# A kernel ordered by a list scheduler: the engine of each PSUM copy made part of the search over orders, and the search continued

## Chip, cores, metric

One NeuronCore of one Trainium2 chip. The metric is the device time of one execution in microseconds (us). TensorE is called PE below, VectorE DVE, ScalarE ACT and GpSimd POOL, as in the profile.

## The reference, cut to what matters

A gated mix of two attention layers over the same x (2048 tokens, 640 wide, 32 heads of 20):

```python
g = sigmoid((x * gate_w).sum(-1, keepdims=True))
a = A(x)   # linear attention: softmax feature maps of q and k, kv = phi_k^T v, normalised by z
b = B(x)   # 4 segments of 512: causal softmax inside a segment, plus a memory M, z of earlier segments
return g * a + (1 - g) * b
```

The arithmetic does not change here: both kernels have the same 3822 matmuls.

## The kernel before: the parts that the argument touches

The program is a graph of 1415 operations, numbered as they are created. A list scheduler in Python orders them when the kernel is built. Each engine then runs its list in that order (in the profile of before VectorE waits 1.76 us for a DMA while a copy whose matmuls ended at 138.9 us stands behind it until 145.08), and the program carries the dependences by semaphores. NUDGE shifts an operation's priority by its number; a smaller `pr` goes earlier.

```python
# Graph.op
o.engs, o.dur, o.fn, o.pr, o.name, o.dma, o.lat = engs, dur, fn, pr + NUDGE.get(len(self.ops), 0.0), name, dma, lat

# Graph.schedule, for every engine e and ready operation o (cut)
s = est(o, e)                      # earliest start: inputs, free PSUM banks, free buffers
if len(o.engs) > 1:                # an operation that two engines could do
    f = s + o.dur[e] - (self.SLACK if e == "pool" else 0.0)
    if any(max(free[x], s) + o.dur[x] < f - 1e-6 for x in o.engs if x != e):
        continue                   # the other engine would be done sooner
# ... of those that can start within DELTA of the earliest, the lowest (pr, idx) wins
```

The only operations with a choice of engine are copies from PSUM, into which this program's matmuls write (`ps` in the profile), to SBUF, where it keeps their operands. There are 113 of them:

```python
def evac(self, n, o, i, W, pr, name="ev", R=(), mode=1):
    op = self.op(("act", "dve"), {"act": d_act(n), "dve": d_dve(n, mode, True)}, None, R=R, W=W, pr=pr, name=name)
    def fn(e):
        if op.stream == "act":
            return e.activation(o(), i(), ACT.Copy)
        return e.tensor_copy(o(), i())
```

Four kinds of operation matter below: the copy of a value tile vA (operation 1113 is that of the 13th tile), the step `pkt1` that reads a transposed key tile pk as soon as its DMA has landed (operation 733), the reduction and the reciprocal of the 14th key tile (1125 and 1126), and the copies of finished output tiles (`out`, for instance 1376). The hole, below, is the idle time of PE at about 144 us, just before the matmuls that need the banks of the 13th value tile.

The softmax here doesn't subtract the row's maximum and nothing guards it: scores larger than these inputs give would overflow.

Of the kernel before, what the change touches and what calls it, by code (L numbers as in the profile page):

```python
# [10 lines left out]
NUDGE = {6: 1.6, 7: 1.65, 8: -2.2, 9: -0.45, 11: -1.7, 19: -3.95, 22: 3, 24: -1.5, 35: -11.8, 36: -2.7, 37: 5.05, 40: 11.15, 62: 0.7, 64: -1.4, 65:  # L11
         -7.8, 66: 0.95, 67: 6.15, 68: 17.2, 69: 9.2, 70: 3.6, 71: 13.15, 72: 2.65, 75: -8.85, 77: 1.3, 93: 4.7, 94: 16.3, 95: -0.65, 97: -1.6, 99:
         -7.9, 101: -10.25, 103: -15.25, 105: 1.1, 106: 9.7, 107: -3.35, 108: -1.55, 109: -0.15, 111: -1.75, 112: 3.45, 113: 0.05, 119: -5.35, 121:
         2.9, 122: 3.2, 124: -5.55, 125: -0.7, 127: 6.1, 129: 3.1, 131: 5.9, 133: -6.55, 135: 5.9, 143: -3.6, 162: -9.4, 163: -4.5, 164: -3.3, 166:
         -9.2, 170: -3.35, 174: 1.85, 179: -5.05, 180: 6, 181: -6.5, 183: -6.3, 187: -3.45, 188: -4.45, 190: -8.2, 192: -2.65, 193: -6.25, 194: -6.6,
         196: -10.35, 200: -0.65, 202: -10.9, 204: -3.1, 205: -2.9, 206: -7.45, 207: -4.25, 208: -8.5, 209: -3.3, 210: -14.45, 211: -7.8, 213: 4.2,
         217: 0.75, 218: -3.2, 219: -10.25, 221: 2.85, 222: -12.25, 223: 42.5, 224: -9.75, 226: -1.55, 230: 0.7, 231: 3.25, 234: -5.6, 235: -1.3, 236:
         5.7, 237: -6.8, 239: -1.75, 241: 6, 243: -0.95, 247: 2.35, 248: 4.6, 249: -4.9, 250: -13.95, 251: 1.2, 252: -9.8, 253: 3.7, 254: 5.35, 256:
         -5.533, 260: -5.3, 269: 1.071, 270: 0.85, 271: -5.1, 273: -4.75, 277: 3.25, 282: 9.4, 283: 6.85, 284: -9.6, 285: 0.95, 286: -8.15, 287: 2.65,
         288: 11.9, 289: -4.05, 290: -0.15, 291: 6.15, 292: 1.452, 293: -1.4, 294: 7.3, 295: 4.35, 296: -1.7, 297: 8.55, 298: -9, 299: -2.3, 300:  # L20
         -5.05, 301: -2.05, 302: 1.6, 303: 1.5, 304: 1.85, 306: -1.25, 307: -4.35, 309: -3.65, 310: 7.4, 311: 0.25, 313: -0.5, 315: 1.4, 319: -1, 321:
         0.7, 322: 3.45, 323: 1.5, 324: -9.9, 325: 4.027, 328: 0.85, 332: 2.7, 333: 5.65, 335: 0.85, 336: 0.5, 337: -2.8, 338: -0.8, 339: 0.85, 341:
         2.8, 344: -3.85, 345: 6, 348: 3.1, 350: 1.35, 352: -1.1, 358: 4.35, 359: 8.25, 360: 4.05, 363: 2.35, 367: 2.55, 368: 8.3, 369: 0.4, 373: 3.9,
         377: -0.7, 383: -0.75, 384: -0.55, 385: -2.35, 386: -0.4, 387: 2.85, 388: 0.05, 389: 3.95, 390: -14.3, 392: 2.6, 397: -7.05, 400: 1.55, 401:
         6.9, 402: 2.35, 403: -2.85, 404: 3.75, 405: -2.9, 407: -0.25, 411: 2.05, 412: 1.75, 413: 3, 415: -0.8, 416: 2.45, 417: -7, 418: -2.65, 419:
         -3.75, 420: -57.2, 421: 10.8, 422: 1.2, 426: 1.55, 430: 3.4, 434: 1.95, 435: 6, 437: -2.15, 438: -1.75, 439: -10.85, 441: -0.8, 445: -0.95,
         446: -2.6, 449: 0.35, 453: 3.75, 455: 10.95, 456: -1.45, 457: -4.15, 458: 7.35, 466: -13.2, 467: -0.9, 468: -2.9, 469: 0.4, 470: 6.4, 471:
         -1.942, 473: -5.4, 475: -1.75, 479: -0.35, 483: -2.15, 484: 0.45, 485: -12, 486: -19.7, 487: -8.75, 488: -8.05, 490: -3.1, 491: -13.85, 492:
         -10.1, 494: 2.6, 498: 3.258, 509: 4.15, 510: -5.5, 511: 9.8, 512: -3.25, 513: -2.6, 514: 8.8, 515: -2.45, 516: 12, 517: 7.6, 518: 1.2, 519:
         -15.923, 521: 0.6, 522: 1.5, 523: -5.35, 524: -0.4, 525: 5.35, 530: -0.035, 531: 0.15, 532: 2.95, 533: -3.8, 534: 0.25, 535: -6.4, 536: 4.8,  # L30
         537: 3.15, 538: 2.672, 539: 14.3, 540: -2, 541: 0.65, 542: 1.4, 543: 6.7, 544: 0.007, 546: 0.5, 547: -9.45, 548: -1.7, 558: 1.65, 559: 4.45,
         561: 4.15, 563: -4.15, 564: 0.1, 565: -1.95, 567: 1.9, 570: 1.8, 571: 0.2, 573: 3.5, 574: 21.8, 576: 4.25, 577: 2.6, 578: 1.5, 579: -9.5,
         581: 3.15, 582: 3.3, 583: 4.4, 584: 10.8, 586: 13.25, 587: 5.9, 590: 0.65, 591: 2.4, 592: 0.35, 594: 10, 596: -4.15, 597: -0.6, 600: 5.4,
         604: -2.4, 605: -0.75, 608: 25.7, 610: -6.8, 611: -6.05, 612: -10.2, 616: -8.4, 619: 6.3, 620: 6.2, 626: -3.8, 627: 3.05, 630: -28.25, 631:
         -13.3, 634: 3, 635: -8.65, 636: 5.15, 638: 2.55, 639: 0.85, 647: 11.35, 649: 1.85, 653: -2.35, 654: -1.35, 658: 3.6, 659: 3.5, 660: -3.322,
         662: -15.35, 664: -3.3, 668: -1.45, 672: 7.55, 673: 10.05, 678: 4.9, 679: -2.05, 683: -2.2, 687: -2.95, 688: 2.05, 690: 10.05, 693: 4.75,
         694: -2.55, 696: -3.55, 698: -2.6, 702: -2.45, 706: -1.65, 707: -6, 710: -8.75, 712: 14.75, 713: -2.8, 715: 3.15, 717: -3.7, 721: 1.45, 722:
         -5.1, 725: -8.9, 726: 0.25, 727: 6.4, 728: 5.1, 733: 0.35, 734: 2.7, 735: 18.4, 736: 8.7, 737: 6.55, 738: 22.45, 739: 0.8, 740: 11.5, 741:
         8.3, 742: 2.2, 743: 7.75, 744: 7.6, 745: -4.95, 746: 5.7, 747: -3, 748: 2.8, 753: 2.45, 755: -0.35, 757: 7.5, 759: 0.674, 760: -6.65, 761:
         0.3, 763: -0.5, 764: 2.35, 765: 7, 767: 3.5, 768: 5.5, 769: 5.75, 770: 2.8, 771: -1.45, 781: 2.2, 784: 0.45, 787: 16.15, 790: -7.7, 791:  # L40
         -0.85, 794: 1.6, 800: 14.35, 801: 7.1, 802: 4.15, 803: 21, 804: 12.15, 805: 6.2, 806: 2.45, 807: 5.2, 809: 18.6, 810: 4.05, 811: 9.2, 812:
         8.95, 813: 19.25, 814: 4.35, 816: 6.15, 817: 9.1, 819: -1.1, 823: -3.9, 827: -1.3, 828: -1.9, 834: 2.15, 835: -5.85, 838: 2.35, 842: 9.2,
         843: -0.45, 845: 54.95, 849: 0.7, 850: -5.8, 853: -1.4, 857: -6.05, 860: 15.5, 861: 3.05, 862: 2.2, 865: 6.6, 867: 26.85, 868: -6, 869: 3.15,
         872: -12.3, 876: 3.95, 877: 4.1, 881: 10.1, 882: 3.85, 883: -1.35, 885: 6.9, 887: 3.35, 891: -1.95, 895: -3.45, 896: -11.95, 900: 6.05, 902:
         -2.5, 903: 12.15, 904: -5.35, 906: -3.85, 910: -10.45, 911: -2.4, 917: 0.05, 919: 7, 921: -0.85, 925: -12.75, 929: 7.15, 930: 6.35, 936:
         1.45, 938: 1.25, 946: 4.95, 951: -2.5, 952: -9.6, 953: -7.2, 955: 4.85, 959: -3.7, 961: -3.5, 962: -2.4, 963: 2.15, 967: -1.85, 968: 14.1,
         969: 6.35, 970: -4.6, 971: 0.5, 972: -3.95, 973: 0.95, 975: -2.55, 976: 14.9, 977: -5.4, 979: 9.25, 981: 0.1, 982: -4.7, 983: -4.75, 984:
         0.85, 985: -7.75, 988: 4.1, 990: -1.75, 991: 1.45, 992: 0.45, 995: 1.8, 999: 0.65, 1001: 9.85, 1003: -0.65, 1004: 4.7, 1005: 5.1, 1006: -6.1,
         1007: 4.2, 1008: 0.85, 1009: 0.4, 1010: 5.15, 1011: 2.85, 1012: 1.35, 1013: 1, 1014: -1.3, 1015: -1.15, 1016: 7.5, 1018: 10.8, 1019: 12.05,
         1020: -0.4, 1021: -9.8, 1022: -3.95, 1023: 0.8, 1024: 5, 1025: 5.85, 1026: -1.05, 1027: 3.6, 1029: -1.9, 1031: 0.3, 1034: 2.6, 1035: 1.45,  # L50
         1036: -10.55, 1037: 3.55, 1038: 12.15, 1040: -0.65, 1041: 5.25, 1042: -0.5, 1045: 0.9, 1047: -3.8, 1048: 8, 1051: 3, 1052: -4.4, 1053: -5.6,
         1054: -1.9, 1055: 1.8, 1056: -0.4, 1058: -2.9, 1059: 1.115, 1061: -0.15, 1062: 2.05, 1063: -1.7, 1064: -3.5, 1065: 5.3, 1066: -0.9, 1067:
         -7.6, 1068: 4.85, 1069: -2.2, 1070: -0.25, 1072: -6.9, 1073: 1.9, 1075: -2.2, 1076: -0.6, 1077: 0.1, 1078: -3.05, 1079: 3.3, 1080: 2.464,
         1081: 1.75, 1083: -1.1, 1084: 1.9, 1087: -3.75, 1088: -8.6, 1090: 5.25, 1091: 2.85, 1092: 2.25, 1095: 1.95, 1097: -5.7, 1098: 1.95, 1101:
         8.85, 1103: 0.4, 1104: 3.4, 1105: -7.75, 1106: -0.15, 1107: -4.85, 1108: -3.45, 1109: 1.55, 1112: 1.85, 1113: 8, 1114: 2.95, 1115: -0.7,
         1116: 5.8, 1118: -1.35, 1119: -1.1, 1120: 0.75, 1123: 0.9, 1127: 7.2, 1129: 3.95, 1130: 0.65, 1131: 1.3, 1133: -4.3, 1134: 1.5, 1136: -2.35,
         1137: 1.7, 1138: 5.9, 1140: 3.05, 1142: 0.35, 1145: 1, 1146: -1.25, 1147: -7.1, 1148: -5.5, 1151: 8.2, 1152: 17.25, 1153: 0.4, 1154: 1.55,
         1155: 8.55, 1156: -2.5, 1157: -8.7, 1158: -2.8, 1161: -4.65, 1168: -4.15, 1170: -3.35, 1171: 7.5, 1173: -3.45, 1175: -3.7, 1176: -5.15, 1177:
# [110 lines left out]
class Graph:  # L169
# [34 lines left out]
    def schedule(self):  # L204
# [147 lines left out]
        while done < n:  # L352
            best = None
            for e in STREAMS:
# [5 lines left out]
                for o in L:  # L360
# [5 lines left out]
                    if len(o.engs) > 1:  # L366
                        f = s + o.dur[e] - (self.SLACK if e == "pool" else 0.0)
                        if any(max(free[x], s) + o.dur[x] < f - 1e-6 for x in o.engs if x != e):
                            continue
# [12 lines left out]
            s, e, o = best  # L382
# [1102 lines left out]
```

## Time and profile before

| | before |
|---|---|
| median of 3 runs | 324.94 us (324.57 to 326.56) |
| profiled run | 326.07 us, span 324.3 us |
| busy PE / ACT / DVE | 299.9 / 256.4 / 237.6 us |
| PE idle in the span | 24.4 us |
| mean granted PE clock | 0.989 of full speed |

Read it so: PE is the busiest engine and its work is fixed, so time can be won only from its idle 24.4 us and from stretches in which its clock is lower (0.50 from 146 to 151 us). The prediction shows the lines.

### The profile page before, as it was taken

The page shows a single profiled execution, that of the slowest core. Times are in us where ns is not written, and L with a number is a line of the kernel's source. Part 1 is how long each engine was busy: PE and PEld are TensorE (multiplying, and loading weights), DVE is VectorE, ACT ScalarE, POOL GpSimd, SP SyncE. Part 2 cuts the span into 40 slices and gives each one's busy share as a digit, 9 for nine tenths or more (in the row PEclk, how much of TensorE's full clock was granted, in tenths as well). Part 3 has the DMA queues.
Part 4 walks back from the last instruction along what each step waited for, and adds up shares of the span by engine and source line. Part 5 has one row for each costly group of instructions (what it writes and reads, how often), then busy time and mean ns, then how long its engine had stood idle before and what let it go on. Part 6 is the DMA issues. An engine that isn't in the chain of part 4 may idle for free.

```text
span 324.3 us, 8898 instructions
## 1 busy us (share of the span) xinstructions
PE 299.9 (92%) x3822; PEld 176.2 (54%) x3822; DVE 237.6 (73%) x468; ACT 256.4 (79%) x309; POOL 107.8 (33%) x169
## 2 busy tenths in 40 slices
PE   7998999899899999759989999999999998888896
PEld 3453565566456656526465455656365564546564
DVE  5536799999999899976999995815774446856460
ACT  4478999987999889695988998778887958476722
POOL 6558113603343423350461232133322403223300
PEclk9999999999999999996999999999999999999999
DMA  7999873626225329962390101762045320311212
GB/s 248 298 211 202 107 125 57 121 68 111 55 40 103 64 49 103 123 96 42 114 173 1 23 2 12 123 132 63 22 42 62 84 60 7 59 51 34 63 23 81
DMA packets 70961, 28.01 MB, mean 86 GB/s; under 512 B 62410, under 2 KB 69002, under 8 KB 70922
## 3 DMA queue, kind: packets, MB, share of 16 engines
q1 hardware_dynamic: 70858, 27.41, 44.9%
q8 instruction: 30, 0.49, 0.6%
q0 software_dynamic: 64, 0.03, 0.2%
q14 instruction: 9, 0.07, 0.1%
HBM read 7.57 MB, written 4.59 MB: 37 GB/s over the span
## 4 chain that ended last, share of the span: by engine, by line
PE 58%; DVE 22%; ACT 15%; issue 2%; DMA 1%; SPq 1%; POOL 1%; DVEq 0%
PE ps L1385 10%; PE ps L889 8%; PE ps L1097 8%; PE ps L1184 5%; ACT exb L1057 5%; PE ps L1033 4%; PE ps L1286 4%; DVE z L1199 4%; ACT ET L1291 3%; PE ps L1386 3%; DVE acc L1211 2%; ACT exb L1046 2%; PE ps L910 2%; PE ps L1232 2%; DVE E L1202 2%; DVE cb L1143 2%
## 5 line engine op out<-in xcount | busy, mean ns | idle before, releaser
L1051 POOL TENSOR_SCALAR_AFFINE_SELECT exb<-exb 128x512 bf16<-128x512 bf16 x96 | 68.8, 718 | 159.7 <-ACT exb L1046 86.9
L1046 ACT ACTIVATE exb<-ps 128x1024 bf16<-128x1024 f32 x64 | 62.1, 1025 | 13.2 <-PE ps L1033 13.0
L1057 ACT ACTIVATE exb<-ps 128x2048 bf16<-128x2048 f32 x32 | 60.0, 1876 | 3.1 <-PE ps L1033 2.9
L1097 PE MATMUL ps<-v1B,exb 128*128 128x42 bf16 (+1 forms) x1280 | 42.5, 182 | 4.8 <-DVE vA L858 2.0
L1097 PEld LDWEIGHTS ps<-v1B,exb 128*128 128x128 bf16 x1280 | 39.7, 97 | 11.4 <-DVE vA L858 2.5
L889 PE MATMUL ps<-xT,WB 128*128 128x512 bf16 x175 | 42.5, 380 | 1.8 <-DVE oB L1138 0.9
L1033 PE MATMUL ps<-qk 20*128 20x128 bf16 (+3 forms) x512 | 31.9, 302 | 4.8 <-ACT exb L1057 2.3
L1066 ACT ACTIVATE exb<-ps 128x2048 bf16<-128x2048 f32 x16 | 30.0, 1877 | 2.1 <-PE ps L1033 2.1
L1070 POOL TENSOR_SCALAR_AFFINE_SELECT exb<-exb 128x512 bf16<-128x512 bf16 x32 | 21.4, 688 | 30.6 <-ACT exb L1066 28.4
L857 ACT ACTIVATE out<-ps 128x640 bf16<-128x640 f32 (+1 forms) x17 | 11.4, 672 | 19.8 <-PE ps L1386 18.2
L889 PEld LDWEIGHTS ps<-xT,WB 128*128 128x128 bf16 x175 | 15.4, 98 | 21.0 <-issue 2.0
L1184 PE MATMUL ps<-WkA,xT 128*128 128x512 bf16 x80 | 24.6, 396 | 2.2 <-ACT exb L1046 1.1
L1191 ACT ACTIVATE E<-ps 128x640 bf16<-128x640 f32 x32 | 22.6, 706 | 3.9 <-PE ps L1185 3.4
L1199 DVE TENSOR_REDUCE z<-E 128x64 f32<-128x1280 bf16 x16 | 23.6, 1477 | 2.1 <-ACT E L1191 1.9
L1291 ACT ACTIVATE ET<-ps 128x512 bf16<-128x512 f32 x40 | 22.9, 600 | 2.7 <-PE ps L1286 2.2
L910 PE MATMUL ps<-WvB,xT 128*128 128x512 bf16 x80 | 23.8, 380 | 0.8 <-DVE oA L1354 0.6
L1202 DVE TENSOR_TENSOR E<-E,z 128x1280 bf16<-128x1280 bf16 x16 | 24.2, 1514 | 0.2
L1286 PE MATMUL ps<-xT,WqA 128*128 128x512 bf16 x100 | 24.0, 380 | 0.3 <-DVE ET L1330 0.2
L1184 PE MATMUL ps<-WvA,xT 128*128 128x512 bf16 x80 | 23.4, 380 | 0.8 <-ACT E L1191 0.8
L1385 PE MATMUL ps<-Wo,oTA 128*128 128x512 bf16 x75 | 22.1, 380 | 1.5 <-ACT exb L1057 1.2
L1385 PE MATMUL ps<-Wo,oTB 128*128 128x512 bf16 x75 | 21.9, 379 | 0.0
L1033 PEld LDWEIGHTS ps<-qk 20*128 20x128 bf16 x512 | 8.9, 92 | 23.2 <-issue 6.2
(137 smaller groups left out, 593.3 us busy)
## 6 DMA issues: line engine op xcount, KB each, us to landing
out_dram<-out SPq DMA_DIRECT2D x15, 160.0 KB, 1.9
scr<-qk SPq DMA_DIRECT2D x16, 120.0 KB
qk<-scr SPq DMA_DIRECT2D x16, 120.0 KB
stq<-in_B_wq_dram SPq DMA_DIRECT2D x5, 160.0 KB, 4.1
WvB<-in_B_wv_dram SPq DMA_DIRECT2D x1, 800.0 KB, 5.4
WvA<-in_A_wqkv_dram SPq DMA_DIRECT2D x1, 800.0 KB, 7.8
Wo<-in_A_wo_dram SPq DMA_DIRECT2D x1, 800.0 KB, 4.8
Wo<-in_B_wo_dram SPq DMA_DIRECT2D x1, 800.0 KB
```

What stands on the lines that cost most here:

```text
L889: r = e.matmul(self.pf(pt, 0, 0, LSEG), lhsT=self.WB[:, w, kc, 128 * c:128 * (c + 1)], rhs=xT[:, kc, LSEG * n:LSEG * (n + 1)], start=(kc = ...
L1033: r = e.matmul(self.pf(pts[i][0], pts[i][1], c0, N), lhsT=qk[32 * i:32 * i + DH, gg, 1, 128 * j:128 * (j + 1)], rhs=qk[32 * i:32 * i + DH, ...
L1046: self.op("act", d_act(1024), lambda e, p=p, pt=pt: e.activation(ex[:, 2 * p:2 * p + 2, off:off + 512], self.pbanks(pt, 0, 2, 512), ACT.Ex ...
L1051: self.op("pool", d_pool(n_el), lambda e: e.affine_select(view(), view(), pattern=pat, compare_op=ALU.is_ge, fill=0.0, base=0, channel_mul ...
L1057: return self.op("act", 1.79, lambda e: e.activation(ex[:, :, off:off + 512], four(pt), ACT.Exp, scale=scale), W=[(pt, i) for i in range(4 ...
L1097: r = e.matmul(self.pf(ad, b, 84 * q2 + 21 * i, w) if n else self.pf(ad, 0, 84 * qi + 21 * i, w), lhsT=ex[:, i, c0:c0 + 128], rhs=vt[:, j, ...
L1184: e.matmul(self.pf(pt, 0, 0, 512), lhsT=l, rhs=W[:, kc, 0:512], start=(kc == 0), stop=(kc == 4))
L1199: self.op("dve", 1.46, lambda e: e.tensor_reduce(rz[:, :], Ev(), axis=AX.X, op=ALU.add), R=[(E, 0), (E, 1)], W=[(rz, "*")], pr=pr, name="Z ...
L1202: self.op("dve", 1.46, lambda e: e.tensor_tensor(Ev(), Ev(), rz[:, :].rearrange("p (h o) -> p h o", o=1).to_broadcast([128, 2 * H, DH]), A ...
L1286: r = e.matmul(self.pf(pt, 0, 0, LSEG), lhsT=self.WqA[:, kc, 128 * c:128 * (c + 1)], rhs=xT[:, kc, LSEG * S:LSEG * (S + 1)], start=(kc == ...
L1291: op("act", d_act(512), lambda e, s=s, ET=ET, pt=pt: e.activation(ET[:, s, :], self.pf(pt, 0, 0, LSEG), ACT.Exp, scale=1.0 - 2.0 * s), W=[ ...
L1385: e.matmul(self.pf(pt, 0, 0, 512), lhsT=l, rhs=self.Wo[:, c, 0:512], start=(c == 0), stop=(c == 9))
```

## The change

The intent: let the search over orders also push each copy to one engine or the other, and search on. The scheduler gets a table BIAS, in us, subtracted from ScalarE's finish when the engine of a copy is chosen; negative values favour VectorE. The whole of it besides the numbers:

```diff
                     if len(o.engs) > 1:
-                        f = s + o.dur[e] - (self.SLACK if e == "pool" else 0.0)
-                        if any(max(free[x], s) + o.dur[x] < f - 1e-6 for x in o.engs if x != e):
+                        b = {o.engs[0]: BIAS.get(o.idx, 0.0)}
+                        f = s + o.dur[e] - b.get(e, 0.0)
+                        if any(max(free[x], s) + o.dur[x] - b.get(x, 0.0) < f - 1e-6 for x in o.engs if x != e):
                             continue
+BIAS = {120: -3.05, 121: -4, 122: -2.5, 124: -0.1, 126: -2.25, 134: -6.75, 145: -3.15, 151: -5.65, 154: -9.2, 308: -3.75, 310: -4.1, 314: -2.65,
+        326: 3.05, 547: -2.75, 754: -1.85, 756: 9.15, 766: 3.85, 772: 2.95, 789: -0.7, 1113: -5.6, 1284: 5.45, 1376: -2.15, 1382: -2.2, 1385: -1.55,
+        1391: -5.8}
 NUDGE = {...   # 722 entries become 749, 120 values differ; among them (cut):
-         421: 10.8, ... 1101: 8.85, ... 1116: 5.8, 1119: -1.1, ... 1127: 7.2, ...
+         421: 13.65, ... 1101: 8.2, ... 1116: 6.7, 1119: 2.6, ... 1122: 22.9, ... 1127: 12, ...
```

## The prediction

> **What bounds the kernel now.** I read the page first, then busy time in stretches of 10 us, then of 1 us, then the timeline of the worst stretch and the chain that ended last. The page's first part:
>
> ```profile
> span 324.3 us, 8898 instructions
> PE 299.9 (92%) x3822; PEld 176.2 (54%) x3822; DVE 237.6 (73%) x468; ACT 256.4 (79%) x309; POOL 107.8 (33%) x169
> ```
>
> TensorE (PE) is busy 299.9 of 324.3 us, and the change touches no matmul. So the change can win only PE's idle 24.4 us, and time lost to a lower clock. Stretches of the trace place the idle time: 1.3 us before the warm-up matmuls and 2.6 us after the last matmul (copy and store of the output, which stay); 5.4 us in 130 to 146; 7.7 us in 200 to 312; the remaining 7.4 us in pieces of 1 to 2 us per 30 us. The one bad place, in rows of start:end, length, then busy us (instructions) of each engine, clock, DMA share, GB/s:
>
> ```profile
> 130.00:140.00 10.00, 7.27 (x113) 4.46 (x110) 9.53 (x18) 7.29 (x8) 2.88 (x5) 1.00 1.09 128
> 140.00:150.00 10.00, 7.33 (x82) 4.01 (x79) 8.05 (x15) 7.07 (x8) 3.77 (x6) 0.75 0.42 78
> 150.00:160.00 10.00, 9.78 (x112) 5.36 (x110) 7.42 (x12) 8.72 (x12) 2.58 (x3) 0.91 0.08 12
> ...
> 144.00:145.00 1.00, 0.00 (x0) 0.00 (x0) 0.97 (x2) 1.00 (x3) 0.58 (x1) 1.00 0.00 0
> 145.00:146.00 1.00, 0.10 (x3) 0.11 (x4) 1.00 (x3) 0.47 (x1) 0.69 (x2) 0.52 0.00 0
> 146.00:147.00 1.00, 1.00 (x30) 1.00 (x30) 1.00 (x1) 0.00 (x0) 0.00 (x0) 0.50 0.00 0
> 151.00:152.00 1.00, 1.00 (x33) 1.00 (x30) 0.00 (x0) 0.81 (x2) 0.03 (x1) 0.57 0.00 0
> ```
>
> PE idles about 2 us at 143.9 to 145.9 and then works at half clock until about 151.9. Half of these 6 us, 3.0 us, is lost to the clock: PE is counted busy there, so this loss lies inside the 299.9. The timeline says what it waited for (start, length, engine, line, what; in brackets the idle time before it and its releaser):
>
> ```profile
> 141.62 0.33 DVE L951 TENSOR_SCALAR tmp<-pk 128x640 bf16<-128x640 bf16 x1 [1.76 <-DMA pk<-qk]
> 143.10 1.47 DVE L1199 TENSOR_REDUCE z<-E 128x64 f32<-128x1280 bf16 x1
> 144.61 0.55 DVE L1201 RECIPROCAL z<-z 128x64 f32<-128x64 f32 x1
> 145.08 0.76 DVE L858 CAST vA<-ps 128x640 bf16<-128x640 f32 x1
> 145.90 0.61 PE ps L1097 x12
> ```
>
> VectorE (DVE) first waited 1.76 us for a transposing DMA, then ran a 1.47 us reduction and a 0.55 us reciprocal, and only then the copy of a PSUM tile whose matmuls had ended at 138.9. The tile held its banks for 7 us; PE needed them for the next attention tile. This is an order fault in DVE's queue, not a lack of VectorE.
>
> The second place is the last third. In the chain that ended last, in order of time:
>
> ```profile
> 249.61 0.70 ACT out L857
> 250.31 1.78 ACT exb L1057
> 265.54 0.70 ACT out L857
> 266.24 1.77 ACT exb L1057
> 298.99 0.70 ACT out L857
> 299.69 1.78 ACT exb L1057
> ```
>
> Three times a copy of a finished output tile on ScalarE (ACT) stands directly ahead of an exponential that the next matmuls wait for. In 260 to 312 DVE has 33.4 us of work in 52 us, so it has room for such copies.
>
> [...] VectorE 823 and 684 ns, ScalarE 703 and 597. So a copy moved to VectorE is some 15% slower, and pays only where ScalarE is what others wait for. [...]
>
> **The change, part by part.** The program is ordered at build time by a list scheduler; NUDGE shifts an operation's priority (higher is later) and the new BIAS makes ScalarE look that many us earlier or later when the engine of a copy is chosen. I numbered the operations of the kernel before as the program creates them, since both tables use these numbers, and noted their engine there.
>
> (a) BIAS has 25 entries. 20 are negative (towards VectorE): 11 of those copies run on ScalarE now (3 of 512 columns, 4 v copies, 4 output copies), 9 run on VectorE already and are only held there. 5 are positive: 3 move from VectorE to ScalarE (two of 512 columns, one 64-partition copy), 2 are held. If all take effect, ScalarE loses 3 x 0.597 + 4 x 0.707 + 4 x 0.703 = 7.4 us and gains 2 x 0.597 + 0.6 = 1.8, net -5.6 (to 250.8). VectorE gains 3 x 0.684 + 8 x 0.823 = 8.6 and loses 2 x 0.684 + 0.417 = 1.8, net +6.8 (to 244.4). Neither sum sets the time; only the places matter. The 4 output copies are those now at 249.61, 265.54, 298.99 and 304.86: three are the chain's lines above. Each can bring the exponential behind it 0.70 us earlier, 2.8 us in all, but PE has other matmuls there: its own waits for these exponentials (line 1057) sum to 3.5 us in the whole run. I count 0.9 us. The first-stage copies (3 q copies and 3 v copies go to VectorE) lie where PE idles 1.1 us in 24.5: 0.2 us.
>
> (b) NUDGE changes 120 entries. One answers to the hole. Operation 1122, the second exponential of the 14th key tile, gets +22.9 (from 0): it goes much later. That tile's reduction and reciprocal, the 1.47 and 0.55 us at 143.10 and 144.61, need it, so they leave their place ahead of the copy (operation 1113, which BIAS holds on VectorE). The copy then starts at about 145.08 - 2.02 = 143.06, which is before PE ran out of work at 143.9. That takes away the wait of 2.0 us, and with it the fall of the clock, 3.0 us: 5.0 us. I weight it with 0.65, since every order before it moves too and the wait for the DMA may come back elsewhere: 3.3 us.
>
> (c) The rest of the nudges (about 35 on QK, PV and query/key projections, about 30 on VectorE's small steps) I can't work out one by one. A search keeps a step only if its own estimate falls; of the 7.4 us of idle time outside the two places and the two ends I give it 0.5 us.
>
> Sum: 0.9 + 0.2 + 3.3 + 0.5 = 4.9 us; 324.9 - 4.9 = 320.0.
>
> **Rivals.** First: the hole only moves. The scheduler's table of durations does not know of the clock, and a DMA that lands late stops VectorE's in-order queue wherever the order puts it. For it: the DMA pk<-qk landed in 2.6 to 4.6 us in this run, while the program plans 3.0. Against it: this is the only fall of the clock in the run. Then the time is 323 to 325. Second: VectorE becomes the bound. In 40 to 140 it is busy 9.0 to 9.9 of each 10 us, and it gets 6.8 us more. Against it: the moved copies lie in the first 35 us, around 160 to 190, and after 245, where it is busy 3.6 to 9.5 of 10, mostly below 8. Then some PE waits for DVE grow, and the time stays at 323 to 326. Third: a broad win, in which the search also halves the 7.7 us in 200 to 312: then 315 to 317.
>
> **Range and chances.** The hole's 5.0 us comes or doesn't: with it 317 to 320, without it 322 to 325. Under 318.4 (2%) needs the hole and over half of one more place: 0.25. Over 331 needs a new fault larger than the hole: 0.03, since PE's work is the same. Range 316 to 324.3.
>
> **What would show it.** PE busy about 3 us lower (296.9), with a clock of 1.00 in every stretch between 130 and 160; no wait of PE for a vA copy longer than 1 us; ScalarE about 251 and VectorE about 244 us; output copies x13 on ScalarE and x4 on VectorE; fewer output copies in the chain. It is wrong if the clock still falls somewhere (the first rival), if PE's waits for VectorE lines sum to clearly more than now (the second), or if the gain comes from stretches that I left at 0.5 us.

Where the recorded text is marked as cut, it set the trace beside statements on copies, clock and banks that no trace or run of this case shows. No term of the forecast's sum was cut: 0.9 + 0.2 + 3.3 + 0.5 = 4.9 us and 324.9 - 4.9 = 320.0 stand as recorded. The four copy times that are left there are from the profile of before, each pair for 640 and for 512 columns. The 3.0 us for the clock are an estimate, half of the 6 us at 0.50, and high by the same profile: the matmuls of line 1184 with 512 columns, a smaller one between each two, start 0.53 us apart at 0.50 (148.8 to 150.4) and 0.27 us apart at 1.00 (140.5 to 141.3), but the first two groups of attention matmuls behind the copy start 0.48 us apart at 0.50 (145.90 and 146.38) and 0.34 us apart in the kernel after at 1.00 (145.55 and 145.89). That the idle 2.0 us brought the fall of the clock was my reading of this one profile, which shows the two together and no more; a_hole2 below tests it.

## The result, and the profile after

| | before | after |
|---|---|---|
| median | 325.26 us (324.57 to 326.56, 4 runs) | 321.37 us (321.19 to 321.40, 4 runs) |
| profiled span | 324.3 us | 319.6 us |
| PE busy / idle | 299.9 / 24.4 us | 297.3 / 22.3 us |
| ACT / DVE busy | 256.4 / 237.6 us | 252.0 / 245.9 us |
| mean granted PE clock | 0.989 | 1.00 |

The ratio of the two is 0.9875 (95% interval 0.9842 to 0.9907). Ratios are the mean time of one kernel's fast runs over that of the other's of the same rounds, so not quite the ratio of the medians quoted. The interval lies clear of 1. The outputs are right.

The page of the kernel after, first part:

```profile
span 319.6 us, 8900 instructions
PE 297.3 (93%) x3822; PEld 174.5 (55%) x3822; DVE 245.9 (77%) x475; ACT 252.0 (79%) x302; POOL 110.5 (35%) x169
```

The span fell by 4.7 us: 2.6 us of PE's busy time (no stretch at half clock any more) and 2.1 us of its idle time. The place that was worst before, in stretches of 10 us (start:end, length, busy us with instructions of PE, weight loads, DVE, ACT, POOL, then clock, DMA share, GB/s), in the kernel after:

```profile
130.00:140.00 10.00, 7.43 (x120) 5.32 (x118) 9.66 (x20) 6.58 (x7) 2.69 (x4) 1.00 1.03 130
140.00:150.00 10.00, 8.50 (x143) 4.89 (x140) 9.86 (x16) 9.93 (x11) 5.91 (x7) 1.00 0.48 82
150.00:160.00 10.00, 9.84 (x101) 4.95 (x97) 9.93 (x16) 9.94 (x13) 4.12 (x4) 1.00 0.34 103
```

The clock stays at 1.00. The idle time at 130 to 140 is as before; that at 140 to 150 is smaller. Its timeline shows what became of VectorE's queue ahead of the vA copy:

```profile
142.43 1.48 DVE L1206 TENSOR_REDUCE z<-E 128x64 f32<-128x1280 bf16 x1
143.94 0.55 DVE L1208 RECIPROCAL z<-z 128x64 f32<-128x64 f32 x1
144.41 0.26 DVE L958 TENSOR_SCALAR tmp<-pk 128x640 bf16<-128x640 bf16 x1
144.59 0.81 DVE L865 CAST vA<-ps 128x640 bf16<-128x640 f32 x1
145.55 0.46 PE L1104 MATMUL ps<-v1B,exb 128*128 128x42 bf16 x12
```

Compare this with the same stretch in the prediction. The reduction and the reciprocal still stand ahead of the copy. What changed its place is the step on pk: it waited 1.76 us for its DMA ahead of everything, and now comes last ahead of the copy, with no wait, since the transfer has landed by then. The copy and the attention matmuls behind it follow at once.

In the last third, a finished output tile is copied on VectorE while ScalarE goes straight to its exponential:

```profile
246.53 0.82 DVE L865 CAST out<-ps 128x640 bf16<-128x640 f32 x1 [2.81 <-PE ps L1393]
246.87 1.88 ACT L1073 ACTIVATE exb<-ps 128x2048 bf16<-128x2048 f32 x1 [0.96 <-PE ps L1040]
```

In the kernel before the same copy took 0.70 us on ScalarE, directly ahead of an exponential. Of the 14 engine changes that the prediction read from the signs of BIAS, 13 came true (operation 124, at -0.1, stayed); 10 copies without an entry changed engine as well.

### The profile page after: what moved, and what is told of

It is laid out like the page before. It is cut to its first block, busy times and chain, and to the rows that moved or that the text cites. A ratio compares the mean times of both kernels' runs of the same rounds, so it can differ in the third digit from the quotient of the medians.

```text
span 319.6 us, 8900 instructions
## 1 busy us (share of the span) xinstructions
PE 297.3 (93%) x3822; PEld 174.5 (55%) x3822; DVE 245.9 (77%) x475; ACT 252.0 (79%) x302; POOL 110.5 (35%) x169
## 4 chain that ended last, share of the span: by engine, by line
PE 54%; DVE 22%; ACT 15%; POOL 3%; DMA 2%; issue 2%; DVEq 0%; POOLq 0%
PE ps L1392 10%; PE ps L1104 8%; PE ps L896 6%; PE ps L1191 5%; PE ps L1293 5%; PE ps L1040 4%; ACT exb L1064 3%; ACT exb L1053 3%; DVE z L1206 3%; DVE E L1209 3%; ACT ET L1298 2%; DMA wphi<-in_A_w_phi_dram 2%; PE ps L1393 2%; ACT exb L1073 2%; PE ps L1354 2%; ACT E L1198 2%
## 5 line engine op out<-in xcount | busy, mean ns | idle before, releaser
L1058 POOL TENSOR_SCALAR_AFFINE_SELECT exb<-exb 128x512 bf16<-128x512 bf16 x96 | 69.9, 730 | 151.7 <-ACT exb L1053 81.4
L1104 PE MATMUL ps<-v1B,exb 128*128 128x42 bf16 (+1 forms) x1280 | 41.7, 181 | 3.0 <-DVE cb L1150 1.0
L1104 PEld LDWEIGHTS ps<-v1B,exb 128*128 128x128 bf16 x1280 | 38.8, 96 | 9.5 <-POOL exb L1058 2.8
L1077 POOL TENSOR_SCALAR_AFFINE_SELECT exb<-exb 128x512 bf16<-128x512 bf16 x32 | 22.9, 736 | 30.5 <-ACT exb L1073 30.5
L1191 PE MATMUL ps<-WkA,xT 128*128 128x512 bf16 x80 | 23.5, 380 | 2.8 <-ACT exb L1053 1.1
L1209 DVE TENSOR_TENSOR E<-E,z 128x1280 bf16<-128x1280 bf16 x16 | 24.9, 1556 | 0.2
L1298 ACT ACTIVATE ET<-ps 128x512 bf16<-128x512 f32 x40 | 22.9, 600 | 2.3 <-PE ps L1293 1.8
L1040 PEld LDWEIGHTS ps<-qk 20*128 20x128 bf16 x512 | 8.9, 92 | 22.9 <-issue 6.7
L864 ACT ACTIVATE out<-ps 128x640 bf16<-128x640 f32 (+1 forms) x13 | 8.6, 663 | 14.9 <-PE ps L1393 13.3
```

The source lines that it names most:

```text
L1040: r = e.matmul(self.pf(pts[i][0], pts[i][1], c0, N), lhsT=qk[32 * i:32 * i + DH, gg, 1, 128 * j:128 * (j + 1)], rhs=qk[32 * i:32 * i + DH, ...
L1058: self.op("pool", d_pool(n_el), lambda e: e.affine_select(view(), view(), pattern=pat, compare_op=ALU.is_ge, fill=0.0, base=0, channel_mul ...
L1104: r = e.matmul(self.pf(ad, b, 84 * q2 + 21 * i, w) if n else self.pf(ad, 0, 84 * qi + 21 * i, w), lhsT=ex[:, i, c0:c0 + 128], rhs=vt[:, j, ...
L1191: e.matmul(self.pf(pt, 0, 0, 512), lhsT=l, rhs=W[:, kc, 0:512], start=(kc == 0), stop=(kc == 4))
L1209: self.op("dve", 1.46, lambda e: e.tensor_tensor(Ev(), Ev(), rz[:, :].rearrange("p (h o) -> p h o", o=1).to_broadcast([128, 2 * H, DH]), A ...
```

## The experiments

Two ways of making them were used. The first edits the tables and lets the scheduler build a new order. The second keeps the order of a kernel and changes only named places: after scheduling, operations are moved within one engine's list, or given to the other engine at the same place, and the lists are merged again under all dependences. Two runs (b_double, a_hole2) instead add work to one operation and leave the order alone. The second way is the one that can tell causes apart, and its diff is:

```diff
         self.schedule()
+        self.rearrange()      # MOVES: ((operations), directly ahead of this one); ENGINES: (operation, engine)
         self.emit()
```

All twelve kernels gave correct results. The three calls ran on three chips. Where a run is compared with the kernel after, that is a comparison across calls. Beside the times I use three marks in each profile: the start of the second memory product (line 965 before, 972 after; about 122 us), that of the third (about 191 us), and the last output copy. They cut the run into a middle part, where the hole lies, and a last part. Each of these figures is from one profile. The same middle part came out as 67.72 us twice (after, a_out_act), and the same last part as 127.70 to 127.72 us four times.

| kernel | median us (range) | clock of the runs | middle part us | last part us |
|---|---|---|---|---|
| before (profiled run, clock fell) | 325.26 (324.57 to 326.56) | see below | 72.22 | 127.70 |
| after | 321.37 (321.19 to 321.40) | 1.00 (profile) | 67.72 | 126.40 |
| b_double | 326.60 (323.15 to 326.67) | 1.00, 0.995 x3 | 68.95 | 127.72 |
| b_zsum_late | 323.62 (323.08 to 325.31) | 1.00 x4 | 69.13 | 127.72 |
| b_pkt1_late | 323.23 (322.70 to 323.62) | 1.00 x4 | 68.60 | 127.72 |
| a_pkt1_early | 322.65 (322.37 to 324.12) | 1.00 x3, 0.994 | 68.87 | 126.49 |
| b_out_dve | 326.62 (324.31 to 328.30) | 0.998, 0.989 x2, 0.99 | 69.09 | 127.15 |
| a_out_act | 322.08 (321.86 to 322.80) | 1.00 x4 (one 0.999) | 67.72 | 127.31 |
| a_undo_both | 323.27 (322.83 to 323.67) | 1.00 x4 | 68.76 | 127.21 |
| a_hole2 | 325.88 (324.19 to 326.15) | 0.989 x2, 0.995 x2 | 72.15 | 126.39 |
| a_fix | 321.17 (320.48 to 323.31) | 1.00 x2, 0.995 x2 | 67.93 | 126.37 |

**What the kernel before did when it ran beside these.** It ran 21 times. In 9 runs the mean clock was 1.00: 322.49 to 324.68 us, mean 323.5. In 6 it was 0.995: mean 325.7. In 6 it was 0.989 or 0.990: 326.0 to 328.2, two of them counted as slow and left out of what follows. So the half clock seen in the profile is not in every run. It differs between runs of the same program. An estimate, if the lower clock is always the 0.50 of the profile of before: a mean clock lower by 0.005 is 0.01 of a run of 322 us at half clock, about 3.2 us, and 0.010 is twice that. The profile of before, at 0.989, shows a stretch of 6.8 us (0.75 over 10 us and 0.91 over 10 us). This was not known when the prediction was written. The hole varies as well: with operation 733 (the step `pkt1` that reads a transposed key tile pk as soon as its DMA has landed) at its old place VectorE waited 1.76 us for the DMA in the profile of before, but 1.00 to 1.14 us in three profiles of the same order whose clock did not fall there (b_double, b_zsum_late, b_out_dve). That a late DMA is what decides about the fall is likely, but not shown. In b_out_dve the order around the hole is that of before with nothing added, so it shows what the hole was in one run at full clock there, 1.07 us and not 2.0:

```profile
142.20 0.33 DVE L951 TENSOR_SCALAR tmp<-pk 128x640 bf16<-128x640 bf16 x1 [1.14 <-DMA pk<-qk]
146.16 0.47 PE L1097 MATMUL ps<-v1B,exb 128*128 128x42 bf16 x12 [1.07 <-DVE vA L858]
```

### b_pkt1_late: the wait for the DMA moved behind, in the kernel before

```diff
+    MOVES = (((1101, 1102, 1125, 1126), 733),)     # chain, chain, reduction, reciprocal go ahead of pkt1
```

> Kernel before, one VectorE order changed: operation 733 (the step on pk that waits for its DMA) goes from ahead of the two chain adds, the reduction 1125 and the reciprocal 1126 to behind them, directly ahead of the copy 1113, as in the kernel after. Theory A (VectorE's stall of 1.76 us on the DMA is what held the copy, and the clock fell because of it): the stall goes, the copy starts near 143.3 instead of 145.08, no half clock, busy TensorE near 297, time 4 to 5 us lower, about 320.5. Recorded theory B (the reduction and the reciprocal ahead of the copy are the cause): little or nothing, 324 to 325. Rival C (the hole moves elsewhere): the half clock comes in another place, 323 to 325.

Measured: 323.23 us, the clock 1.00 in all four runs; PE's wait for the vA copy fell to 0.6 us, from 2.0 in the profile of before and 1.07 in that of b_out_dve:

```profile
145.46 0.47 PE L1097 MATMUL ps<-v1B,exb 128*128 128x42 bf16 x12 [0.60 <-DVE vA L858]
```

The fall of the clock went, as theory A says. But the time is only 0.2 us under that of the kernel before at full clock (323.5), and the middle part 0.35 us under that of b_double and 0.49 us under that of b_out_dve, which both have before's order there at full clock. The number I gave, 320.5, was too low: I had counted a clock loss that 9 of 21 runs do not have and the hole of one profile in which the DMA was late.

### b_zsum_late: the recorded mechanism, made by hand

```diff
+    MOVES = (((1113,), 1125),)                     # the vA copy goes ahead of the reduction and the reciprocal
```

> Kernel before, one VectorE order changed: the copy 1113 goes ahead of the reduction 1125 and the reciprocal 1126, which is the mechanism of the recorded prediction; the stall on the DMA stays ahead of it. Theory B: the copy starts near 143.06, the 2.0 us wait of TensorE and the half clock go, 320 to 321. Theory A says the same here, since any 2 us ahead of the copy will do; only if the clock does not depend on this gap (rival) does it stay at 323 to 325.

Measured: 323.62 us at 1.00 in all four runs. The copy and the matmuls did come early:

```profile
142.22 0.82 DVE L858 CAST vA<-ps 128x640 bf16<-128x640 f32 x1
142.96 1.47 DVE L1199 TENSOR_REDUCE z<-E 128x64 f32<-128x1280 bf16 x1
143.80 0.46 PE L1097 MATMUL ps<-v1B,exb 128*128 128x42 bf16 x12
```

PE's wait for the copy was gone and the clock did not fall. VectorE's wait for the DMA was 1.11 us here, so by b_out_dve it is a hole of about 1.1 us that was closed, not one of 2.0. Yet the middle part is 69.13 us, no shorter than b_double's 68.95 and b_out_dve's 69.09. The win was given back within a few microseconds, in waits of PE for VectorE's products, of which this is the longest:

```profile
PE ps L1033 <- DVE cb L1143: 1.0, 1, 1.0
```

VectorE has the same work in either order and is busy 9.0 to 9.9 of every 10 us from 40 to 140. Putting PE's next need first here only moved the wait to the need after it. What may help there, as I argue it, is to end VectorE's own idle time (the 1.11 us), which moving the pk step does (no wait ahead of it in the timeline of b_pkt1_late) and this edit does not. The 0.35 to 0.49 us of b_pkt1_late fit this, but they are differences of single profiles.

### b_double: useless matmuls in the hole

```diff
-                    for kc in range(NCH):
+                    for kc in list(range(NCH)) * (2 if (n, w, c) == (3, 1, 0) else 1):
                         r = e.matmul(self.pf(pt, 0, 0, LSEG), lhsT=self.WB[:, w, kc, ...
```

> Kernel before, order unchanged; the five matmuls of the projection that ends just before the hole (operation 755) are done twice into the same bank, the second pass overwriting the first, so the result is the same. 1.08 us of useless matmul fills about half of the 2.0 us hole. If the half clock after the hole comes from that idle time and costs 3.0 us: the clock stays at 1.00 and the time falls by about 3 us, to 322, although work was added. If the fall of the clock has another cause, or costs nothing: 325 to 326.

Measured: one run of 323.15 us at 1.00 and three of 326.57 to 326.67 at 0.995. Half of the expectation failed: the added matmuls did not keep the clock up, since it fell in three of four runs. The profile caught the run without a fall. There the DMA was early enough that the added matmuls filled the whole hole (PE had no wait for the vA copy), so how much of it they filled in the other three, and where the clock fell, is not known. The run is useful in two ways. Its order is that of the kernel before, so its profile shows that order at full clock: 68.95 us in the middle part against 72.22 with the fall and a longer wait for the DMA (1.76 against 1.00 us). And one program with runs at both mean clocks shows how much longer those with a fall took: 326.62 - 323.15 = 3.5 us. How much of it is the clock alone is not shown, since the DMA may have been later in them too.

### a_pkt1_early: the wait for the DMA put back, in the kernel after

```diff
+    MOVES = (((733,), 1101),)
```

> Kernel after, one VectorE order put back: operation 733 ahead of the two chain adds, as in the kernel before. Theory A: VectorE stalls on the DMA for 1 to 2 us again, the copy comes that much later, TensorE gets a hole of 1.5 to 2 us, the clock falls for about 6.8 us, time 4 to 5 us up, 325 to 326. If the new order as a whole makes this place harmless (rival): 321.4 to 322.

Measured: 322.65 us, 1.3 us more than the kernel after; three runs at 1.00, one at 0.994 (324.12). The stall, the late copy and PE's wait are all back, smaller than in the profile of before:

```profile
141.95 0.33 DVE L958 TENSOR_SCALAR tmp<-pk 128x640 bf16<-128x640 bf16 x1 [0.73 <-DMA pk<-qk]
145.54 0.76 DVE L865 CAST vA<-ps 128x640 bf16<-128x640 f32 x1
146.45 0.46 PE L1104 MATMUL ps<-v1B,exb 128*128 128x42 bf16 x12 [0.87 <-DVE vA L865]
```

The middle part grew by 1.15 us, the last part by 0.1. So the place of this one operation is worth about 1.2 us at full clock in the new order, more than the 0.35 to 0.49 us in the old one. One of the four runs fell. The expected 4 to 5 us were wrong, as the clock fell in one of four runs only.

### b_out_dve and a_out_act: the four output copies alone

```diff
+    ENGINES = ((1376, 'dve'), (1382, 'dve'), (1385, 'dve'), (1391, 'dve'))     # b_out_dve; 'act' in a_out_act
```

> Kernel before, order unchanged, only the four output copies 1376, 1382, 1385, 1391 go from ScalarE to VectorE at the same place of the order. Recorded step (a): 0.9 us less; in the trace the time between the copy at 249.6 and the next output copy, 10.62 us before and 9.29 us after the change, falls to about 9.3 to 9.8, and the rest of the last third hardly changes. Rival (the copies are hidden anyway): the distance stays at 10.6 and the time at that of before. The time of whole runs will hardly show it, since the runs of the kernel before spread over several us with the half clock; I read the trace.

> Kernel after, only the same four output copies put back on ScalarE. Step (a): 0.9 to 1.3 us more, 322.3 to 322.7, and the distance between the second and third output copy after 243 us grows from 9.29 to about 10.6. Rival (hidden anyway): 321.2 to 321.5. The runs of the kernel after spread by 0.2 us, so here the time can tell.

Measured: with these four back on ScalarE the kernel after takes 322.08 us, 0.7 us more, and its last part grows by 0.91 us (127.31 against 126.40). Given to VectorE in the kernel before they shorten its last part by 0.55 us (127.15 against 127.70), while the time of whole runs is buried under the clock: three runs of b_out_dve were at 0.99 (326.53 to 328.30 us, which says nothing of the copies). In the fourth, the profiled one (0.998), the clock was lower only in the last 1.3 us, behind all matmuls. It took 324.31 us, so the 0.55 us cannot be seen in its time either: its last output copy was followed by 3.3 us, where the other profiles have 2.5 to 2.6. The distance that I had named as the place to look hardly moved: 10.42 against 10.62 us in the kernel before, 9.54 against 9.29 in the kernel after. The gain is spread over the copies, as four small steps.

### a_undo_both: do the two pieces explain the change?

```diff
+    MOVES = (((733,), 1101),)
+    ENGINES = ((1376, 'act'), (1382, 'act'), (1385, 'act'), (1391, 'act'))
```

> Kernel after with both known pieces undone: operation 733 (waits for the DMA) back ahead of the chain adds, and the four output copies back on ScalarE; all else as after. Singly they cost about 1.3 us (322.65 median) and 0.7 us (322.08). If these two are what the change gained apart from the clock: 323.3 to 323.5 in runs at a clock of 1.00, which is where the kernel before stands in such runs (mean 323.5), and some runs with a fallen clock. If the rest of the new order is worth something by itself: below 322.8.

Measured: 323.27 us, all four at 1.00. That is 1.9 us more than the kernel after, close to the sum of the two single costs (1.3 + 0.7 = 2.0), and 0.2 us under the mean of the kernel before at full clock (323.5). With the spread of those nine and these four runs the 0.2 is uncertain by about 0.6 us. So by the times of whole runs the two pieces explain the change apart from the clock, and what the other hundred nudges and engine changes add is too small to see. The marks do not quite agree. With both pieces undone the last part is still 0.5 us and the middle part 0.2 to 0.3 us shorter than in before's order at full clock (127.21 against 127.72, 68.76 against 68.95 and 69.09). So the rest of the new order gained about 0.7 us behind the first mark. Ahead of it the profiles of the new order are no better (first mark at 121.9 to 123.3 us, in the old order at 121.9 to 123.1), and their scatter is too large to say whether it lost as much there. The clock did not fall in these four runs, so what else of the new order keeps it up is not shown by this run.

### a_hole2: the hole opened on purpose

```diff
-        self.evac(640, lambda: v[:, :], ..., name="vA_ev")
+        ev = self.evac(640, lambda: v[:, :], ..., name="vA_ev", R=self.xk(1) if t == 12 else ())
+        if t == 12:                                   # operation 1113
+            copy = ev.fn
+            def slow(e):
+                for k in range(4):                    # 4 reductions of 512 into a scratch column each
+                    e.tensor_reduce(self.slow[:, k:k + 1], xT[:, k, LSEG:2 * LSEG], axis=AX.X, op=ALU.add)
+                return copy(e)
+            ev.fn = slow
```

> Kernel after with useless VectorE work of about 2.4 us (four reductions of 512 elements) directly ahead of the copy 1113, to open the old hole on purpose. VectorE is busy all through this stretch, so about 2.4 us are lost in any case: 323.8 without a fall of the clock. If a hole of some 2 us makes the clock fall: [...] 325.5 to 327, at a mean clock of 0.995 or 0.99 in most runs. If the clock does not depend on the hole: 1.00 in all runs.

The cut passage gave lengths of the slow clock and what they would cost, not all of them shown by a run of this case; the 325.5 to 327 are the 323.8 with that cost added. The 2.4 us can be worked out, as an estimate, from the profile of before: a reduction of 1280 elements takes 1.477 us there (line 1199), so four of 512 some 2.4.

Measured: 325.88 us, and the clock fell in all four runs (0.989 twice, 0.995 twice), where the kernel after has 1.00. In the profiled run PE waited 2.29 us for the copy, and then:

```profile
145.00:150.00 5.00, 2.71 (x48) 1.97 (x47) 4.97 (x9) 2.55 (x3) 1.76 (x3) 0.72 0.00 0
150.00:155.00 5.00, 4.67 (x68) 3.02 (x66) 2.51 (x8) 3.35 (x4) 0.63 (x1) 0.60 0.37 69
155.00:160.00 5.00, 4.61 (x42) 2.43 (x40) 4.93 (x9) 4.70 (x6) 0.64 (x1) 1.00 0.00 0
```

If the lower clock is 0.50, 0.72 over 5 us is 2.8 us at half clock and 0.60 is 4.0: 6.8 us together by this estimate, the same length as in the profile of before. For the 0.50: the group of 16 attention matmuls (line 1097 before, 1105 here) takes 0.78 us behind the hole in both profiles, and 0.56 us at 1.00 in that of after. The middle part grew by 4.4 us, of which 2.4 are the added work (2.45 us in the trace) and the other 2 are put down to the slow clock. So the clock fell in all four runs with the hole put back (2.29 us in the profiled one, with gaps of 0.25 and 0.42 us ahead of it) and in none of the four of the kernel after; I take the hole for the cause.

### a_nobias, a_oldnudge, a_drop126: the tables apart

```diff
-BIAS = {120: -3.05, ...}
+BIAS = {}                      # a_nobias: nudges of after alone

-NUDGE = {... of after ...}
+NUDGE = {... of before ...}    # a_oldnudge: biases of after alone

-BIAS = {... 124: -0.1, 126: -2.25, 134: -6.75, ...}
+BIAS = {... 124: -0.1, 134: -6.75, ...}     # a_drop126: one entry less
```

> Kernel after with an empty BIAS table, the new NUDGE kept, reordered by the scheduler. If the choice of engines carries the gain: 323 to 325. If the nudges carry it: 321 to 322. Since the nudges were searched together with the biases, some loss is likely whatever the cause: I say 322.5.

> Kernel after with the NUDGE table of before: the BIAS table alone added to the kernel before. If the engines carry the gain: 321 to 322.5. If the nudges carry it, or both only work together: 323.5 to 326. I say 324.

> Kernel after with one entry of BIAS taken out, that of operation 126 (a copy of 512 columns at about 15 us), rescheduled. If entries are separate gains, each worth a few tenths: 321.4 to 322. If the tables hold only as a whole, as the runs with one table alone suggest: far slower, 330 to 365, by holes and half clocks all along.

Measured: 351.53, 372.21 and 365.88 us. The first two expectations were far off. Neither table carries the gain; each without the other costs 30 to 51 us against the kernel after, and taking one entry of 25 out costs 44.5 us. Two lines of the page of a_drop126 show the last third of the run (40 slices, tenths of busy time and of the clock):

```profile
PE   8997999998999977689989999889897698763586
PEclk9999999999999999899999999899996579955579
```

PE is 6 to 8 tenths busy in many slices, and its clock is down to 5 tenths in four of the last ten slices. In the built orders the reason can be seen: without entry 126, 23 copies take another engine than in the kernel after, and only 54 of PE's 348 operations keep their position. An early change shifts all that follows, and the numbers of the later entries no longer fit. Of the 25 entries, five when taken out singly (120, 151, 314, 772, 1113) leave the scheduler without any legal next step, so no program is built, and five others (121, 124, 310, 326, 754) change no engine. Entry 126 is at the far end of the rest: in orders built again, and not run, nine entries taken out singly change the engine of one to three copies, and six, 126 among them, that of 8 to 23. So "what is the BIAS worth" is no question that a run without BIAS can answer.

### a_fix: three more moves by hand

```diff
+    MOVES = (((98,), 158), ((1114,), 1115), ((238,), 1036))
```

> Kernel after with three moves in VectorE's order, each from a wait of TensorE of about 1 us for a VectorE copy or product that stood behind work nobody waited for: the weight copy 98 ahead of four small scalings (wait of 1.10 us at 32.9), the product 238 ahead of a reduction (0.89 us at 85.1), the reduction 1114 behind the product that frees the banks (1.14 us at 133.3). If such waits are real time: up to 3 us less, 318.4 to 320.5. If VectorE's total work bounds the stretch from 40 to 170 us, the waits only move, as in the kernel before with its copy moved ahead: 320.8 to 321.5. I say 320.5.

Measured: two runs at 1.00 of 320.48 and 320.49 us, two at 0.995 of 323.31 and 321.86; median 321.17. In the runs at full clock it is 0.9 us faster than the kernel after (321.19 to 321.40), under a third of the 3.1 us of waits that it removed from the places named. In half of its runs the clock fell, which did not happen in the four runs of the kernel after, and that eats the gain: the mean is 321.5. I do not count it as a better kernel. Some of its waits were moved, as the rival said. Of these two the first grew (0.6 us in the kernel after) and the second is new:

```profile
PE ps L1104 <- DVE qk L865: 1.0, 2, 0.8
PE ps L1191 <- DVE qk L865: 0.9, 1, 0.9
```

## Why the prediction was right, and where its steps were not

The time (321.37 against 320.0, range 316 to 324.3): right. The time lies in neither of the two stretches that were named, 317 to 320 with the hole closed and 322 to 325 without: the hole closed, and was worth less. The steps in turn:

**Part (a), output copies: right.** Recorded 0.9 us; 0.91 us of the last part and 0.7 us of the time when undone alone in the kernel after, with no other change. The copies fell to x13 on ScalarE and x4 on VectorE as said, and the chain lost those three pairs of lines. The 0.2 us for the first stage were not seen: at the mark at 122 us the profiles of the new order are not ahead of the old ones.

**Part (b), the hole: right that it closes, wrong by which edit, and too large where it closes.** The step that failed is "Operation 1122 ... gets +22.9 ... so they leave their place ahead of the copy". They did not. ScalarE's list still has 1122 directly behind the same two neighbours, because a priority decides only among operations that could start at nearly the same time (within DELTA, 0.12 us), and there was no rival for it to yield to. Orders built again (no runs) settle it. Without the entry of 1122 the kernel after has the same order on every engine. The kernel before with only the nudge of 1101 changed, from 8.85 to 8.2, changes six places, all on VectorE, and has 733 directly ahead of the copy. As far as these orders tell, the edit that closed the hole is thus that of 1101, the first chain add, whose `pr` falls from 22.66 to 22.01 and so below the 22.34 of 733. The scheduler's own estimate stays the same with it (322.6 us), so this step was not chosen for the hole: that it closed is, by the prediction's working, luck. The cause of the late copy is the place of operation 733, whose own nudge did not change. The shown line "141.62 ... [1.76 <-DMA pk<-qk]" held it; I put it down as a wait and looked for a remedy at the two operations behind it. The size: 5.0 us was the sum of 2.0 and 3.0. The runs give about 1.2 us for the order at full clock (a_pkt1_early). The wait was 1.07 us in the full-clock profile of b_out_dve and not 2.0, and a wait of PE in this stretch, where VectorE is full, is not time by itself (b_zsum_late: about 1.1 us of wait removed, no gain at full clock). So "not a lack of VectorE" was wrong too. For the clock they give an average, not 3.0 us: the 19 fast runs of before have a mean of 324.9 us, those at full clock 323.5, so falls cost 1.4 us on average. Together 2.6 us, against my weighted 3.3. That all of the 1.4 us belongs to this hole is argued, not shown. For it: with the hole closed or shortened by hand in the kernel before the clock stayed up in 8 of 8 runs (b_pkt1_late, b_zsum_late), and a hole of 2.3 us brought the fall back in 4 of 4 (a_hole2). Against it: with 733 put back in the new order only 1 of 8 runs fell (a_pkt1_early, a_undo_both), where PE's wait was 0.87 and 0.76 us.

**Part (c), the rest: 0.5 us recorded, 0.2 us measured, uncertain by 0.6** (a_undo_both against before at full clock; about 0.7 us by the marks, if the first 122 us are left out). The sum of what was measured is 0.7 + 1.2 + 1.4 + 0.2 = 3.5 us; the medians differ by 3.9 us. The difference is within the spread; how often the clock fell in before's four runs of that call is not on record.

**The rivals.** The first (the hole moves) is refuted for the change, but its reason holds: the scheduler does not know of the clock, and a_fix shows an order that is better by its waits and worse by its clock. The second (VectorE bounds) is not what happened to the time: PE's waits for VectorE sum to 11.4 us before and 11.7 after. But the 2.0 us for the vA copy are gone from that sum, so its other waits grew by about as much, and this is why the middle part gave so little. The third did not come.

What stays open: why b_double, with work put into the hole, fell more often than the kernel before, where in a_fix the clock fell, and which of the new order's parts keeps the clock at 1.00 in every run of the kernel after.

## What to carry to other kernels

When an order is made by a greedy scheduler with tuned offsets, undo a change at the place in the final order, not in the tables: a part of the tables can build quite another order. Build that order and compare it before spending a run on it; here it would have shown that the nudge of 1122 moves nothing. When one in-order engine is full over a stretch, look whether another engine's waits for it are time that can be won one by one (here none of 1.1 us, and 0.9 of 3.1), and try to end that engine's own stalls, here a step that waited for a transfer (1.76 us) ahead of work that was ready; undoing that cost about 1.2 us in the kernel after. And when the runs of a kernel spread by more than the gain, sort them by the granted clock before comparing.
